# Attention's projections as float32 matmuls on two 64-row halves, from q and k also laid out transposed

## The chip, the cores and the metric

One core of a Trainium2 chip runs the whole kernel. The metric is device time in microseconds (us), the median of several runs. The core has a matrix engine (TensorE, PE in the rows; its weight loads are PEld), a vector engine (VectorE, DVE), a scalar engine (ScalarE, ACT), GpSimd (POOL) and SyncE (SP), whose queue issues most DMAs. Matmuls write to PSUM, eight banks of 128 x 512 float32; everything else lives in SBUF.

## The reference

Three stages, one after the other: attention with random features, a gated MLP over all tokens (MoE 1), and a top-1 mixture of eight experts (MoE 2).

```python
# attention: q, k, v [4, 8, 576, 64], omega [128, 64], float32
scale = 1 / sqrt(sqrt(64))
def phi(x):                                   # x = q * scale or k * scale
    h = einsum('bhsd,md->bhsm', x, omega) - sum(x * x, -1) / 2
    return exp(h - max(h, -1)) / sqrt(128)
kv = einsum('bhsm,bhsd->bhmd', k_p, v); z = sum(k_p, 2)
out = einsum('bhsm,bhmd->bhsd', q_p, kv) / (einsum('bhsm,bhm->bhs', q_p, z) + 1e-06)
# MoE 1: x [2304, 512]; w_a, w_b [512, 1536], w_out [1536, 512], given as float64
x = ((x @ w_a) * (x @ w_b)) @ w_out
# MoE 2: per token the expert with the largest cosine similarity,
#        out = gate * (relu(x @ w1[e]) @ w2[e]), w1 [8, 512, 1024], w2 [8, 1024, 512]
```

## The kernel before, in words

**Attention** is cut into 36 jobs, 18 of k and 18 of q. A job is 128 tokens x 8 (head, part) pairs, 1024 rows of 64 numbers; two neighbouring jobs share one load of 512 KB, and four jobs ("left") hold the last 64 tokens of two batch entries. `attention` runs over slots t; in slot t job t+2 is transposed and squared (`j_T`), job t+1 is projected and exponentiated (`j_proj`, `j_exp`), job t adds to the sums over keys (`j_kv`) or has its features transposed (`j_pT`), job t-1 is multiplied with these sums (`j_out`), and job t-2, where it ends a pair, is transposed for MoE 1 (`j_xT`). The loads of a job are called LEAD = 5 slots ahead.

In `j_T`, TensorE turns four blocks of 128 x 128 (L349), ScalarE copies them out scaled as float32r (L351), and VectorE makes the remainder (L352); GpSimd squares the tokens (L356) and folds the squares twice (L358). In `j_proj`, each of four blocks is multiplied with omega, two copies of it on a block diagonal of 128 x 256, as three float32r products (L595 to L597): both high parts, high with low, low with high. VectorE then takes the maximum of 512 columns (L377, two per job), adds the squares (L378) and forms the exponent's bias (L379), for each half of the job by itself; ScalarE makes eight exponentials (L390).

Beside attention, the float64 weights of MoE 1 are converted to float32 in 36 parts (L235, L236, L238, L240: ScalarE, VectorE, VectorE, GpSimd), 24 of them paced over the slots. **Early chunks:** ND = 5 of the 12 column chunks of MoE 1's first unit are multiplied inside attention, at slots TS = 28, 30, ..., 36 (step TD = 2), by `chunk_early` (splits of the weights, L574, L577) and `ab_mm` (24 matmuls; L609, L611).

**Order.** In attention a scheduler orders the instructions of each engine; each engine then runs its list strictly in that order, and SP too. From the first chunk after the early ones on, the order is as written. **Memory** in SBUF comes in slots of a few sizes: "ab" and "wo" (12 each: loads, converted weights), "c4" (4 of 4 KB: xT, xn, later split weights), "x6", "c2" and others. A new tile waits until the last reader of an older tile in its buffer is done.

The functions that the change touches, with the line numbers that the profile shows:

Of the kernel before, what the change touches and what calls it, by code (L numbers as in the profile page):

```python
# [20 lines left out]
VW = 66  # L21
# [18 lines left out]
ND = 5  # L40
TS = 28
TD = 2
# [38 lines left out]

class Later:
    """the engines, their instructions put in a queue for Kern.pump"""
# [17 lines left out]
class Kern:  # L101
    def __init__(s, tc, ctx, q, k, v, omega, w_a, w_b, w_out, emb, tau, w1, w2, cst, ids, ident, tri, out):
        s.tc, s.nc, s.out = tc, tc.nc, out
        s.q, s.k, s.v, s.omega = q, k, v, omega
# [22 lines left out]
    def pump(s, n):  # L127
        """the next n instructions of the queue, up to a barrier; a stage puts its own in its place"""
# [14 lines left out]
    # on-chip memory: slots of few sizes, shared by the phases  # L143
# [81 lines left out]
    def conv_ops(s):  # L225
        """float32 nearest to each float64 (in float32's range), a third of a chunk at a time"""
# [56 lines left out]
    def p0_consts(s):  # L283
        """omega^T twice on the diagonal, in two parts"""
        nc = s.nc
        bd = s.c2([128, 2, 128], F32, "bd")
        nc.vector.memset(bd, 0.0)
        pt = s.psum("O", "omT")
        nc.tensor.transpose(pt[:, :128], s.om2.rearrange("p a d -> p (a d)"), s.ident)
        for i in range(2):  # L290
            nc.vector.tensor_copy(out=bd[64 * i:64 * i + 64, i], in_=pt[64 * i:64 * i + 64, :128])
        s.omh = s.one([128, 256], F32R, "omh")
        s.oml = s.one([128, 256], F32R, "oml")
        s.split(s.omh, s.oml, bd.rearrange("p a m -> p (a m)"))
# [193 lines left out]
    def attention(s):  # L488
# [18 lines left out]
        for t in range(-2, J + 3):  # L507
# [15 lines left out]
            if c:  # L523
                s.hi_()
# [874 lines left out]
```

## Time and profile before

| | us |
|---|---|
| median of three runs | 920.87 (916.97 to 922.1) |
| profiled execution, span | 917.3 |
| TensorE busy in it | 847.3 (92%) |
| VectorE | 599.2 (65%) |
| ScalarE | 452.0 (49%) |
| GpSimd | 349.9 (38%) |
| TensorE's mean granted clock | 0.979 of 2.4 GHz |

The page gives no other time of the profiled execution than its span, which lies 3.6 us under the median and inside the spread of the runs. Busy shares over the whole span mix attention (some 200 us) with the two MoE stages, whose limits differ; the page's 40 slices show VectorE at 8 and 9 tenths in the first eight slices and at 3 to 8 after, TensorE at 9 nearly everywhere after them. A record of TensorE lasts longer than the distance to the next one, since matmuls overlap: the distance between two starts is what a matmul costs in a stream.

### The profile page before, as it was taken

The page shows a single profiled execution, that of the slowest core. Times are in us where ns is not written, and L with a number is a line of the kernel's source. Part 1 is how long each engine was busy: PE and PEld are TensorE (multiplying, and loading weights), DVE is VectorE, ACT ScalarE, POOL GpSimd, SP SyncE. Part 2 cuts the span into 40 slices and gives each one's busy share as a digit, 9 for nine tenths or more (in the row PEclk, how much of TensorE's full clock was granted, in tenths as well). Part 3 has the DMA queues.
Part 4 walks back from the last instruction along what each step waited for, and adds up shares of the span by engine and source line. Part 5 has one row for each costly group of instructions (what it writes and reads, how often), then busy time and mean ns, then how long its engine had stood idle before and what let it go on. Part 6 is the DMA issues. An engine that isn't in the chain of part 4 may idle for free. (4 is left out here: it accounts for less than half of the span.)

```text
span 917.3 us, 15916 instructions
## 1 busy us (share of the span) xinstructions
PE 847.3 (92%) x5784; PEld 763.8 (83%) x5784; DVE 599.2 (65%) x1295; ACT 452.0 (49%) x1039; POOL 349.9 (38%) x332
## 2 busy tenths in 40 slices
PE   7889897999899999999999999999899799998991
PEld 6778786898798899899889989989688698887880
DVE  6899999858956866874885687588547432225310
ACT  4789887665445546555555545655431321114210
POOL 6676877304315125222512421341404433333330
PEclk9999999999999999999999999999899899999996
DMA  9674853203200000000000004300214732122110
GB/s 235 183 199 123 240 152 121 74 8 118 114 1 0 36 1 1 1 36 1 1 36 1 1 0 103 117 1 37 60 55 142 262 98 64 50 62 63 61 48 24
DMA packets 68359, 67.20 MB, mean 73 GB/s; under 512 B 27552, under 2 KB 56608, under 8 KB 68096
## 3 DMA queue, kind: packets, MB, share of 16 engines
q1 hardware_dynamic: 62784, 52.90, 19.2%
q0 software_dynamic: 5440, 12.68, 4.6%
q8 instruction: 63, 1.03, 0.5%
q14 instruction: 72, 0.59, 0.2%
HBM read 55.88 MB, written 9.68 MB: 71 GB/s over the span
## 5 line engine op out<-in xcount | busy, mean ns | idle before, releaser
L660 POOL TENSOR_TENSOR trp<-y,en 128x512 f32<-128x512 f32 x60 | 89.2, 1508 | 138.2 <-ACT y L635 91.1
L1034 PE MATMUL p_h<-xth,w1t 128*128 128x256 f32 (+1 forms) x512 | 101.6, 294 | 8.4 <-DVE w2t L563 4.9
L562 ACT CAST hh<-h 128x384 fp32r<-128x384 f32 x72 | 36.9, 513 | 141.7 <-DVE h L611 141.7
L563 DVE TENSOR_TENSOR abl<-ab,abh 128x1024 fp32r<-128x1024 f32 x67 | 84.7, 1264 | 20.9 <-ACT abh L562 20.8
L597 PE MATMUL pB<-xuh,abl 128*128 128x384 f32 x288 | 96.9, 336 | 0.0
L390 ACT ACTIVATE p<-pj,nb 128x128 f32<-128x128 f32 x288 | 80.0, 397 | 26.0 <-DVE nb L379 14.8
L1034 PEld LDWEIGHTS p_h<-xth,w1t 128*128 128x128 f32 x512 | 83.4, 194 | 9.4 <-issue 9.2
L595 PE MATMUL pA<-xuh,abh 128*128 128x384 f32 x268 | 90.2, 336 | 0.0
L597 PE MATMUL pA<-xuh,abl 128*128 128x384 f32 x268 | 89.9, 335 | 0.3 <-DVE abl L563 0.3
L596 PE MATMUL pA<-xul,abh 128*128 128x384 f32 x268 | 90.0, 336 | 0.0
L595 PE MATMUL pB<-xuh,abh 128*128 128x384 f32 x268 | 89.5, 334 | 0.0
L596 PE MATMUL pB<-xul,abh 128*128 128x384 f32 x268 | 89.5, 334 | 0.0
L611 DVE TENSOR_TENSOR h<-pB,a 128x384 f32<-128x384 f32 x72 | 39.7, 551 | 69.5 <-PE pB L597 44.9
L1034 PE MATMUL p_h<-xtl,w1t 128*128 128x256 f32 (+1 forms) x256 | 75.0, 293 | 0.0
L653 DVE CUSTOM_DVE_ANT_0 trv<-y,en 128x512 bf16<-128x512 f32 x60 | 72.2, 1203 | 1.0
L627 PE MATMUL pO<-woh,hh 128*128 128x512 f32 x216 | 65.0, 409 | 7.7 <-ACT woh L562 7.7
L1014 ACT ACTIVATE hT<-p_h 128x512 fp32r<-128x512 f32 (+1 forms) x42 | 22.5, 537 | 98.2 <-PE p_h L1034 86.7
L562 ACT CAST abh<-ab 128x1024 fp32r<-128x1024 f32 x67 | 70.2, 1048 | 0.6 <-PE pB L596 0.6
L1019 DVE SCALAR_TENSOR_TENSOR hT<-p_h,hT 128x256 fp32r<-128x256 f32 (+2 forms) x52 | 25.2, 504 | 68.2 <-ACT hT L1014 47.4
L627 PE MATMUL pO<-woh,hl 128*128 128x512 f32 x216 | 63.8, 404 | 2.8 <-DVE hl L563 2.8
L563 DVE TENSOR_TENSOR hl<-h,hh 128x384 fp32r<-128x384 f32 x72 | 40.4, 561 | 34.8 <-ACT hh L562 34.8
L627 PE MATMUL pO<-wol,hh 128*128 128x512 f32 x216 | 62.7, 399 | 0.0
(233 smaller groups left out, 2142.4 us busy)
## 6 DMA issues: line engine op xcount, KB each, us to landing
stg<-in_moe_w_a_dram SPq DMA_DIRECT2D x12, 512.0 KB, 4.3
stg<-in_moe_w_b_dram SPq DMA_DIRECT2D x12, 512.0 KB, 3.4
stg<-in_moe_w_out_dram SPq DMA_DIRECT2D x12, 512.0 KB, 3.6
st<-in_moe_w_dram SPq DMA_DIRECT2D x12, 512.0 KB, 8.2
st<-in_moe_w_dram SPq DMA_DIRECT2D x24, 256.0 KB, 4.4
yd<-y SPq DMA_DIRECT2D x6, 792.0 KB, 3.7
v<-in_v_dram SPq DMA_DIRECT2D x16, 256.0 KB, 6.1
q<-in_q_dram SPq DMA_DIRECT2D x8, 512.0 KB, 5.1
```

The lines of the kernel that those rows point to most:

```text
L390: s.nc.scalar.activation(out=s.p_[j][:, 4 * half + n], in_=pj[:, n * M:n * M + M], func=ACTF.Exp, bias=nb[:, n:n + 1])
L562: s.nc.scalar.copy(out=hi, in_=src)
L563: s.nc.vector.tensor_tensor(out=lo, in0=src, in1=hi.bitcast(F32), op=ALU.subtract)
L595: mm(out=out, lhsT=ah, rhs=wh, start=st, stop=False)
L596: mm(out=out, lhsT=ah, rhs=wl, start=False, stop=False)
L597: mm(out=out, lhsT=al, rhs=wh, start=False, stop=sp)
L611: nc.vector.tensor_tensor(out=h, in0=pp[1][:, :N], in1=a, op=ALU.mult)
L627: s.nc.tensor.matmul(out=s.po[j], lhsT=a[:, j * 128:j * 128 + 128], rhs=b, start=st, stop=sp)
L653: nc.vector.tensor_tensor_reduce(out=tr, in0=y[:, j, :DM], in1=s.en[:, e], scale=1.0, scalar=0.0, op0=ALU.mult, op1=ALU.add, accum_out=dt[ ...
L660: nc.gpsimd.tensor_tensor(out=tr, in0=y[:, j, :DM], in1=s.en[:, e], op=ALU.mult)
L1019: nc.vector.scalar_tensor_tensor(out=v, in0=pv[:, a - k0:b - k0], scalar=0.0, in1=h, op0=ALU.max, op1=ALU.subtract)
L1034: return lambda: nc.tensor.matmul(out=out, lhsT=a, rhs=b, start=st, stop=sp, skip_group_check=True)
```

## The change

The host now hands over more: `laid` gives q and k as before by token (contiguous per partition), and also transposed (`qta`, `kta`, `qtb`, `ktb`): on partitions 0 to 63 the 64 numbers of each head's even tokens, on 64 to 127 those of the odd ones (for the left tokens: of even and odd heads), tokens along the row. v comes with its columns of ones, omega transposed, twice one below the other.

On the core the transposes, the float32r copies and their remainders, and omega's splits are gone. `j_proj` multiplies, for each of four blocks and each half r of the rows, `kt[64r:64r+64]` (64 x 128, stationary) with `omr[64r:64r+64]` (64 x 128, moving) as one native float32 matmul, the two halves into two PSUM banks. The bias is formed once for all eight rows of a job, after both maxima. The token tiles of q and k, needed for the squares only, now take c4 buffers. ND, TS and TD go from 5, 28, 2 to 6, 18, 3: early chunks at slots 18, 21, ..., 33. `ab_mm` writes its product over its input, and the last preparation of the expert embeddings comes after the conversion in a step, not before.

```diff
-ND = 5
-TS = 28
-TD = 2
+ND = 6
+TS = 18
+TD = 3
...
+def laid(q, k, v, omega):
...
+    def tr(x):
+
+        a = x[:, :, :512].reshape(B, H, 2, 128, 2, D).transpose(0, 2, 4, 5, 1, 3)
+        c = x[:, :, 512:].reshape(2, 2, 4, 2, 64, D).transpose(0, 3, 5, 2, 1, 4)
+        return np.ascontiguousarray(a.reshape(8, 128, H * 128)), np.ascontiguousarray(c.reshape(2, 128, 512))
...
+        s.omr = s.one([128, M], F32, "omr")
+        s.first = s.ab([128, H * 128], name="kt")
+        n = H * 64
+        nc.sync.dma_start(out=s.omr, in_=s.om)
+        nc.sync.dma_start(out=s.first[:, :n], in_=s.x_in["kt"][0][0, :, :n])
+        nc.sync.dma_start(out=s.first[:, n:], in_=s.x_in["kt"][0][0, :, n:])
         nc.sync.dma_start(out=s.ident, in_=ident)
...
+        s.nc.vector.tensor_scalar(out=s.omr, in0=s.omr, scalar1=SCALE, scalar2=None, op0=ALU.mult)
+
+    def load_part(s, what, where, i):
+        left = where == "left"
+        if (what, where, i) == ("kt", 0, 0):
             return s.first
...
+        src = s.x_in[what][1][i] if left else s.x_in[what][0][2 * where + i]
+        if what in "qk":
+            t = s.c4([128, src.shape[-1]], F32, what)
         else:
+            t = (s.wo if left else s.ab)([128, src.shape[-1]], name=what)
+        s.nc.sync.dma_start(out=t, in_=src)
         return t
...
-        for what in ("kv" if kind == "K" else "q"):
+        for what in (("kt", "k", "v") if kind == "K" else ("qt", "q")):
...
-        pt = s.psum("O", "pT")
-        for n in range(4):
-            nc.tensor.transpose(pt[:, n * 128:n * 128 + 128], x[:, n], s.ident)
-        t = s.c4([128, 2, 512], F32R, "xT")
-        s.hi_ = lambda: nc.scalar.activation(out=t[:, 0], in_=pt, func=ACTF.Copy, scale=SCALE)
-        s.lo_ = lambda: nc.vector.scalar_tensor_tensor(
-            out=t[:, 1], in0=pt, scalar=SCALE, in1=t[:, 0].bitcast(F32), op0=ALU.mult, op1=ALU.subtract)
...
+        pj = [s.psum("A", "pj") for _ in range(2)]
+        for n in range(4):
+            c = slice(n * 128, n * 128 + 128)
+            for r in range(2):
+                g = slice(64 * r, 64 * r + 64)
+                nc.tensor.matmul(out=pj[r][:, c], lhsT=t[g, c], rhs=s.omr[g], start=True, stop=True, skip_group_check=True)
+        return pj
...
+    def j_bias(s, j):
+
+        stt = s.nc.vector.scalar_tensor_tensor
+        mx = s.mx_.pop(j)
+        ss = s.sq_[j].rearrange("p (n r) -> p r n", r=2)
+        nb = s.t("nb", 4, [128, 2, 4], F32, "nb")
+        stt(out=mx, in0=ss, scalar=-SCALE * SCALE / 2, in1=mx, op0=ALU.mult, op1=ALU.add)
+        stt(out=nb, in0=ss, scalar=-SCALE * SCALE / 2, in1=mx, op0=ALU.mult, op1=ALU.subtract)
+        return nb
...
+            if b:
+                s.j_max(b, 0, pj)
                 fill()
+                s.j_ssq(b)
+                s.j_max(b, 1, pj)
+                nb = s.j_bias(b)
+                fill()
+                for half in range(2):
+                    s.j_exp(b, half, pj, nb)
...
-        h = s.c15([128, N], F32, "h")
-        nc.vector.tensor_tensor(out=h, in0=pp[1][:, :N], in1=a, op=ALU.mult)
-        return h
+        nc.vector.tensor_tensor(out=a, in0=pp[1][:, :N], in1=a, op=ALU.mult)
+        return a
```

How the order of instructions moves, at three places. First TensorE's list over a q job and a k job in the middle of attention, before (pT: transposes of k or q; pj: projections; ppT: transposes of the features; ou: products with the sums; kv: sums over keys):

```order
L597 MATMUL pj<-omh,xT 128x256 x2
L595 MATMUL pj<-omh,xT 128x256
L596 MATMUL pj<-oml,xT 128x256
L597 MATMUL pj<-omh,xT 128x256
L450 MATMUL ou<-kvs,pT 64x65 x8
L420 MATMUL kv<-v,p 64x65 x12
L450 MATMUL ou<-kvs,pT 64x65 x8
L420 MATMUL kv<-v,p 64x65 x12
L349 MATMUL pT<-ident_t,q 128x128 x4
L595 MATMUL pj<-omh,xT 128x256
L596 MATMUL pj<-oml,xT 128x256
L597 MATMUL pj<-omh,xT 128x256
```

Now, at a like place (pxT: transposes for MoE 1):

```order
L368 MATMUL pj<-omr,kt 128x128 x8
L438 MATMUL ppT<-ident_t,p 128x128 x8
L486 MATMUL pxT<-ident_t,xn 128x128 x8
L368 MATMUL pj<-omr,qt 128x128 x8
L455 MATMUL ou<-kvs,pT 64x65 x8
L425 MATMUL kv<-v,p 64x65 x8
L455 MATMUL ou<-kvs,pT 64x65 x8
L425 MATMUL kv<-v,p 64x65 x8
L368 MATMUL pj<-omr,kt 128x128 x8
```

The four transposes and twelve projections of a job have become eight projections on half the rows, which stand between full transposes and products on half the columns. The count at a row's end is that of the program; a float32 product is two rows in the trace.

Second, VectorE's list over a little more than one job in the middle, before (cv: conversion of weights; rr, xn: division of the result):

```order
L377 TENSOR_REDUCE mxh<-pj 128x4 x2
L378 SCALAR_TENSOR_TENSOR mxh<-ssq,mxh 128x4
L352 SCALAR_TENSOR_TENSOR xT<-pT,xT 128x512
L379 SCALAR_TENSOR_TENSOR nb<-ssq,mxh 128x4
L378 SCALAR_TENSOR_TENSOR mxh<-ssq,mxh 128x4
L238 SCALAR_TENSOR_TENSOR cv<-stg,cv 128x512
L379 SCALAR_TENSOR_TENSOR nb<-ssq,mxh 128x4
L236 TENSOR_SCALAR cv<-stg 128x512
L384 TENSOR_REDUCE ssq<-sq 128x8
```

Now:

```order
L374 TENSOR_REDUCE mxh<-pj 128x4 x2
L263 TENSOR_SCALAR cv<-stg 128x512
L382 SCALAR_TENSOR_TENSOR mxh<-ssq,mxh 128x8
L469 TENSOR_SCALAR rr<-ou 128x4
L383 SCALAR_TENSOR_TENSOR nb<-ssq,mxh 128x8
L265 SCALAR_TENSOR_TENSOR cv<-stg,cv 128x512
L470 RECIPROCAL rr<-rr 128x4
L469 TENSOR_SCALAR rr<-ou 128x4
L471 TENSOR_TENSOR xn<-ou,rr 128x2x128
```

The remainder (L352) is gone, and of four small operations with the squares two are left, each on eight columns; other work stands between them.

Third, SP's queue, near the last load of k. Before, with what each waits for (stg: float64 weights; DMAHW: an older DMA's queue entry):

```order
L220 DMA stg<-in_moe_w_b_dram 128x4x256 [waits DMAHW0_49,DVE_49,Activation_49]
L223 DMA stg<-in_moe_w_out_dram 128x1024 [waits DMAHW1_49,DVE_49,Activation_49]
L309 DMA q<-in_q_dram 128x8x128 [waits DMAHW2_49,PE_49]
L309 DMA k<-in_k_dram 128x8x128 [waits DMAHW3_49,PE_49,Pool_49]
L307 DMA v<-in_v_dram 128x8x64 [waits DMAHW4_49,PE_49,Pool_49]
L307 DMA v<-in_v_dram 128x8x64 [waits DMAHW5_49]
L220 DMA stg<-in_moe_w_a_dram 128x4x256 [waits DMAHW6_49,DVE_49,Activation_49]
```

Now:

```order
L323 DMA kt<-in_kta_dram 128x1024 [waits DMAHW6_49,PE_49]
L323 DMA v<-in_va_dram 128x1056 [waits DMAHW7_49,PE_49]
L247 DMA stg<-in_moe_w_a_dram 128x4x256 [waits DMAHW0_49,DVE_49]
L217 DMA cst_t<-in_cst_dram 128x161 [waits DMAHW1_49]
L247 DMA stg<-in_moe_w_b_dram 128x4x256 [waits DMAHW2_49,DVE_49,Activation_49]
L250 DMA stg<-in_moe_w_out_dram 128x1024 [waits DMAHW3_49,DVE_49,Activation_49]
L218 DMA ids_t<-in_ids_dram 128x36 [waits DMAHW4_49]
L247 DMA stg<-in_moe_w_a_dram 128x4x256 [waits DMAHW5_49,DVE_49,Activation_49]
L323 DMA k<-in_ka_dram 128x1024 [waits DMAHW6_49,Pool_49]
```

The token tile k, which used to be the matmul's operand and to be issued right behind q, now waits for GpSimd alone and stands behind four loads of weights; kt and v go ahead of them.

## Rows read from the trace of the kernel before

**Rows 1.** Windows: length, busy us PE PEld DVE ACT POOL, clock, DMA share, GB/s.

```profile
0.00:13.50 13.50, 8.51 (x37) 7.25 (x37) 7.21 (x18) 2.99 (x5) 6.75 (x13) 1.00 0.95 198
13.50:32.80 19.30, 17.50 (x231) 14.81 (x232) 14.60 (x44) 13.80 (x48) 13.82 (x20) 1.00 1.02 279
32.80:139.60 106.80, 95.40 (x1276) 85.92 (x1274) 105.37 (x293) 92.06 (x268) 79.69 (x85) 0.98 0.60 171
139.60:187.50 47.90, 41.84 (x447) 38.38 (x446) 43.68 (x107) 33.58 (x91) 22.67 (x22) 0.96 0.28 86
...
262.00:900.00 638.00, 612.76 (x3379) 553.38 (x3377) 373.89 (x749) 269.61 (x558) 206.60 (x174) 0.99 0.15 49
```

**Rows 2.** Timeline of ScalarE, jobs 5 and 28: start, us, instruction, idle before.

```profile
32.76 2.19 ACT L390 ACTIVATE p<-pj,nb 128x128 f32<-128x128 f32 x8
...
139.58 1.14 ACT L390 ACTIVATE p<-pj,nb 128x128 f32<-128x128 f32 x4 [0.56 <-DVE nb L379]
```

**Rows 3.** Groups by line, VectorE, 0 to 202.4: busy us, mean ns | idle before.

```profile
L352 DVE SCALAR_TENSOR_TENSOR xT<-pT,xT 128x512 fp32r<-128x512 f32 x36 | 24.4, 679 | 1.5 <-ACT xT L351 1.4
L379 DVE SCALAR_TENSOR_TENSOR nb<-ssq,mxh 128x4 f32<-128x4 f32 x72 | 24.1, 338 | 0.1
...
L378 DVE SCALAR_TENSOR_TENSOR mxh<-ssq,mxh 128x4 f32<-128x4 f32 x72 | 21.4, 300 | 0.0
...
L577 DVE TENSOR_TENSOR abl<-ab,aby 128x512 fp32r<-128x512 f32 x5 | 4.4, 888 | 0.0
L577 DVE TENSOR_TENSOR aby<-ab,aby 128x512 fp32r<-128x512 f32 x5 | 3.9, 774 | 0.3 <-ACT aby L574 0.3
L611 DVE TENSOR_TENSOR h<-pB,a 128x384 f32<-128x384 f32 x5 | 2.8, 552 | 11.0 <-PE pB L597 11.0
```

**Rows 4.** Line L379: ns least/median/most, first and last start, shape.

```profile
L379 DVE SCALAR_TENSOR_TENSOR nb<-ssq,mxh x72: 119/161/1241, 12.5 to 187.6; 128x4 f32<-128x4 f32 x72
```

**Rows 5.** Timeline of VectorE: the remainder and its successor.

```profile
182.87 0.68 DVE L352 SCALAR_TENSOR_TENSOR xT<-pT,xT 128x512 fp32r<-128x512 f32 x1
183.47 0.15 DVE L379 SCALAR_TENSOR_TENSOR nb<-ssq,mxh 128x4 f32<-128x4 f32 x1
```

**Rows 6.** Groups by line, ScalarE, 0 to 202.4: the copy of the transposes.

```profile
L351 ACT ACTIVATE xT<-pT 128x512 fp32r<-128x512 f32 x36 | 23.6, 656 | 3.9 <-PE pT L349 3.9
```

**Rows 7.** Timeline of TensorE: kv, an early chunk and a job, MoE 1's begin.

```profile
103.00 0.64 PE L420 MATMUL kv<-v,p 128*64 128x65 f32 x16
103.47 0.64 PE L450 MATMUL ou<-kvs,pT 128*64 128x65 f32 x16
...
175.51 0.42 PE L595 MATMUL pA<-xuh,aby 128*128 128x384 f32 x1
...
179.84 0.60 PE L349 MATMUL pT<-ident_t,q 128*128 128x128 f32 x4
180.19 0.37 PE L595 MATMUL pj<-omh,xT 128*128 128x256 f32 x1
...
181.58 0.28 PE L597 MATMUL pj<-omh,xT 128*128 128x256 f32 x1
181.79 0.69 PE L450 MATMUL ou<-kvs,pT 128*64 128x65 f32 x16
182.40 0.66 PE L433 MATMUL ppT<-ident_t,p 128*128 128x128 f32 x4
182.99 0.69 PE L450 MATMUL ou<-kvs,pT 128*64 128x65 f32 x16
...
202.48 0.42 PE L595 MATMUL pA<-xuh,abh 128*128 128x384 f32 x1
```

**Rows 8.** Waits of TensorE, 20 to 175 and after 200: us, times, longest.

```profile
PE pA L597 <- DVE aby L577: 3.3, 1, 3.3
...
PE pO L627 <- DVE hl L563: 2.8, 1, 2.8
```

**Rows 9.** DMA issues, 0 to 200: size, median us from issue to landing.

```profile
q<-in_q_dram SPq DMA_DIRECT2D x8, 512.0 KB, 5.1
```

More of the change, by code (lines that the diff above doesn't have):

```diff
@@ L354, in j_T @@
+        x = s.src[kind.lower(), where, i]
+        if where != "left":
+            x = x[:, 512 * (i % 2):512 * (i % 2) + 512]
         sq = s.t("trp", 2, [128, 8, D], F32, "sq")
-        sqb = sq.rearrange("p (n c) d -> p n (c d)", c=2)
-        nc.gpsimd.tensor_tensor(out=sqb, in0=x, in1=x, op=ALU.mult)
+        nc.gpsimd.tensor_tensor(out=sq.rearrange("p c d -> p (c d)"), in0=x, in1=x, op=ALU.mult)
         for w in (32, 16):
             nc.gpsimd.tensor_tensor(out=sq[:, :, :w], in0=sq[:, :, :w], in1=sq[:, :, w:2 * w], op=ALU.add)
-        s.xT_[j] = t
@@ new lines, in j_max @@
+    def j_max(s, j, r, pj):
+        if j not in s.mx_:
+            s.mx_[j] = s.t("mxh", 4, [128, 2, 4], F32, "mxh")
+        s.nc.vector.tensor_reduce(out=s.mx_[j][:, r], in_=pj[r].rearrange("p (h m) -> p h m", m=M), axis=AX.X, op=ALU.max)
+    def j_bias(s, j):
[6 more added lines that the diff above has]
+        return nb
@@ L385, in j_ssq, with j_exp @@
         s.sq_[j] = ss
-    def j_exp(s, j, half, pn):
-        pj, nb = pn[:2]
-        for n in range(4):
+    def j_exp(s, j, half, pj, nb):
+        for n in range(4 * half, 4 * half + 4):
+            m, r = divmod(n, 2)
             s.nc.scalar.activation(
-                out=s.p_[j][:, 4 * half + n], in_=pj[:, n * M:n * M + M], func=ACTF.Exp, bias=nb[:, n:n + 1])
+                out=s.p_[j][:, n], in_=pj[r][:, m * M:m * M + M], func=ACTF.Exp, bias=nb[:, r, m:m + 1])
     def j_kv(s, j, half):
@@ L399, in j_kv @@
             if where == "left":
+                v = v.rearrange("p (h d) -> p h d", d=VW) if n == 4 * half else v
                 s.kv_mm(2 * i, h, p[0:64, n], v[0:64, h])
@@ L488, in attention @@
     def attention(s):
-        for n in ("src", "xT_", "sq_", "p_", "later", "kvp", "kvn", "kvs", "pT_", "xn_"):
+        for n in ("src", "sq_", "p_", "mx_", "later", "kvp", "kvn", "kvs", "pT_", "xn_"):
             setattr(s, n, {})
@@ L518, in attention @@
                 s.j_T(c)
-            pj = [s.j_proj(b, half) for half in range(2)] if b else None
+            pj = s.j_proj(b) if b else None
             for f in s.xT_evac:
@@ L555, in attention @@
             if a:
-                for d in (s.xT_, s.sq_, s.p_):
+                for d in (s.sq_, s.p_):
                     d.pop(a)
@@ L1383 @@
     nc = bacc.Bacc("TRN2", target_bir_lowering=False, num_devices=1)
-    given = {}
+    given = laid(*(np.asarray(inputs[name]) for name in ("q", "k", "v", "omega")))
     for name in _INS:
```

108 lines of the change are left out of this document (28 added, 80 removed).

## The prediction

> **What bounds the kernel now.** I first cut the span into stretches with the table of windows [rows 1]. The cuts are where ScalarE begins the exponentials of attention's jobs 0, 5, 28 and 35 (the timeline shows the two in the middle, 23 jobs apart [rows 2]) and where the last attention matmul hands over to MoE 1, at 202.5 [rows 7]. From 262 on TensorE is busy 96% of the time, and little less between the two: a microsecond taken from its work, or from the time before 202.5, is a microsecond of the result. Before 202.5 it is not TensorE that sets the pace. From 32.8 to 139.6 VectorE is busy 105.4 of 106.8 us, TensorE 95.4, ScalarE 92.1, GpSimd 79.7. A job takes 106.8 / 23 = 4.64 us there, and VectorE's work is what fills it. From 139.6 to 187.5 VectorE is again the busiest (43.7 of 47.9), with TensorE close (41.8). In the last 15 us before 202.5 two early chunks of MoE 1 lie beside the end of attention.
>
> Next I read which VectorE work that is, from the groups by line [rows 3]. Of the instructions that a job needs, the change takes L352 (0.679 us) and half of L378 and L379 (0.300 and 0.338 each). The latter are 128x4 operations; L379 takes 0.161 in the median, but up to 1.24 [rows 4].
>
> **VectorE, removed.** Per job one L352 and two small ones go: 0.679 + 0.300 + 0.338 = 1.32 us. Records overlap their neighbours: L352 at 182.87 has its successor at 183.47, 0.60 us later for a record of 0.68 [rows 5]. So I take 0.07 off each: 1.1 us per job. The two that stay become 128x8; eight elements for four I cost at nothing, since the time of these is start-up and waiting, not elements. Were each longer by half of 0.161, it would be 0.16 us per job back. The memsets of v go too, and the preparation of omega at the start.
>
> **ScalarE, removed.** L351, 0.656 us per job [rows 6], about 0.6 net.
>
> **TensorE, removed and added.** In a run of TensorE's timeline [rows 7] the four transposes of a job take 180.19 - 179.84 = 0.35 us, and the twelve 128x256 projections 181.79 - 180.19 = 1.60: 1.95 per job go. The new ones are 8 native float32 matmuls of 64 x 128 stationary on 128 columns. The trace of before has no such shape. The nearest rows are the kv and ou products, float32 on 64-column halves: 8 of them in the program are 16 passes in the trace, so float32 takes two passes, and 16 passes go from 103.00 to 103.47, 0.029 us per pass of 65 columns. If row halves run side by side as these column halves do, 128 columns take 0.029 x 128 / 65 = 0.058, and 16 passes 0.92 us. If each waits for the other, the nearest row is a full-array float32 transpose of 128 columns, 4 in 182.99 - 182.40 = 0.59 with a change of shape in it, some 0.125 each: 16 make 2.0 us. I take 0.95, nearest to the products that are also two passes on half the array. Changes of shape: 181.58 to 181.79 is 0.21 where the eleven before it are 1.39 / 11 = 0.13 apart, so 0.08 each; now there are about five per pair of jobs where there were two or three, 0.1 us per job. Net TensorE per job: 1.95 - 0.95 - 0.1 = 0.9 less, or 0.15 more by the upper bound. The Trainium skill, TensorEngine Tiling (Array Packing), Key Properties, says that a change of tiling mode drains the engine, which speaks against rows mixed with columns like this; the trace agrees in kind, with 0.08 as its size, and a drain of a whole record (0.28) in each of five would make 0.5 us per job more.
>
> **GpSimd** keeps all its work (squares and their sums on it as before).
>
> **Moved: early chunks.** One costs TensorE 179.84 - 175.51 = 4.33 us; VectorE 0.888 + 0.774 + 0.552 = 2.2, some 2.0 net [rows 3, 7]; ScalarE two operations. Before, the five come at slots 28 to 36: three in 139.6 to 187.5, two after. Now six come at slots 18 to 33: three before job 28, three from there to job 35, none after.
>
> **Loads.** q and k come twice, 9.4 MB more, but the row pieces are 2 to 4 KB long. DMA is full only up to 32.8 us, at 198 and 279 GB/s [rows 1]. Up to job 5 the queue now has 5.0 MB ahead; at 279 GB/s 18 us, under the 25 that the work itself needs below. So I cost them at nothing there. Later the share was 0.60 and 0.28.
>
> **The sum, stretch by stretch, against the profiled 917.3 us.**
> - To 13.5: the two splits of omega and the transposes are gone; the chain is now k's landing, three operations of GpSimd, the bias. 10.5 us instead of 13.5: gain 3 (1 to 5).
> - Jobs 0 to 4, 19.3 us: TensorE 17.5 - 5 x 0.9 = 13, GpSimd 13.8, ScalarE 13.8 - 3 = 10.8, VectorE 14.6 - 5.5 = 9.1. I take 14.5: gain 4.8 (2 to 6).
> - Jobs 5 to 27, 106.8 us: VectorE 105.4 - 23 x 1.1 + 3 x 2.0 = 86; TensorE 95.4 - 23 x 0.9 + 3 x 4.33 = 88; ScalarE 92.1 - 23 x 0.6 = 78 and six operations more; GpSimd 79.7. Four engines are within 10% of each other, so none will be busy 99% as VectorE was. With TensorE 93% busy, 95 us: gain 12 (6 to 18).
> - Jobs 28 to 34, 47.9 us: TensorE 41.8 - 7 x 0.9 = 35.5, VectorE 43.7 - 7.7 = 36, the same three chunks. The old wait of 3.3 us for a chunk's split [rows 8] can come again, and on SP the load of k for job 28 now stands behind weight loads that wait for the conversion. I take 43: gain 5 (1 to 10).
> - From job 35: two chunks (8.7 us) leave 6.3; what stays is a chain (transposes, copy, product, reciprocal, transposes) that nothing covers any more. I take 9: gain 6.
> - After: one chunk fewer, 4.3 less, but its cover goes. 12 conversions now fall on four steps, not five, and VectorE is the later one there already (TensorE waits 2.8 us for hl [rows 8]). I take 3 us back: gain 1.3.
>
> Together 32 us: 917.3 - 32 = 885.3. The median of the runs, 920.87, is 3.6 above the span; so 889.
>
> **The rivals.**
> *The row halves do not run side by side.* For it: no row here shows two row halves at once. Against: column halves do run so [rows 7]. At 2.0 us per job TensorE has 0.15 more work per job than before; jobs 5 to 27 then have 95.4 + 3 + 13 = 112 us of TensorE records, and gain nothing; the jobs before and after keep about 3 + 1 + 1, the end 5, the rest 1: 10 us, 911. The Trainium skill, TensorE: Matmul & The Clock Gate, section LDWEIGHTS (loading the stationary operand), says that a load of weights takes as long as its columns, whatever the rows; an estimate by its figure, 128 / 1.2 = 107 ns, makes 16 loads one after the other 1.7 us, near this rival; no row here shows loads of this shape.
>
> *GpSimd's collisions eat the gain.* For it: L379 runs from 0.119 to 1.24 us [rows 4], so VectorE's small operations wait for something; GpSimd's work stays, in less time, at 80 of 95 us in the middle. If that middle takes 101 and each later stretch 2 more: 32 - 6 - 6 = 20 gained, 901.
>
> *The four engines overlap better.* TensorE and VectorE then set 89, 38 and 7 in the three last stretches of attention: 6 + 5 + 2 more, 45 gained, 876.
>
> *Slower: the four c4 buffers.* The token tiles of q and k now share these with xn; 16 loads wait on SP for GpSimd's squares of an older tile, and kt, v and the weights queue behind them. If a load is issued too late for its job, a landing of 5.1 us [rows 9] stands open. Seven of them cancel the gain; ten give 51 - 32 = 19 us more, 940. Against: each load is called five jobs ahead, some 20 us, and a buffer comes round after 5.3 slots.
>
> **How the numbers follow.** The forecast, 889, has 0.50 (by itself 878 to 900); better overlap, 876, 0.19; the halves in turn, 911, 0.12; collisions, 901, 0.13; late loads, 940, 0.06. The range, 868 to 912, leaves out the last and the far ends of the others. 0.5%, 4.6 us, is about what a measurement can tell (the three runs spread 5.1 us). Faster by more: all of the first, second and fourth, most of the third: 0.90. Same 0.04, slower 0.06.
>
> **What would show it.** The new projections: 16 passes in about 1 us, pairs starting together (right), or 2 us (the first rival). VectorE in the middle stretch below 95% busy and a job under 4.2 us. No L351 and L352. The exponentials of job 35 near 163 us and MoE 1 at about 172 instead of 202.5. TensorE waiting for kt or qt from DMA, or GpSimd for k or q, by more than 10 us in total, would be the last rival. The forecast is wrong if MoE 1 begins later than 185 or if the time after it grows by more than 6 us.

## The result and the profile after

The changed kernel takes 932.16 us (median of 4 runs, 929.89 to 932.53), the kernel before 919.77 in runs on the same chip: a ratio of 1.012, with a 95% interval of 1.0091 to 1.015. It is slower, and the forecast was 889. Of all runs one, of lean_chunks, counts as slow (1.7% above the fastest of its kernel), and it is left out below. The profiled execution has a span of 930.3 us, 13.0 more than before's 917.3, and a mean clock of 0.954 (0.979 before).

The table of windows of the changed kernel (columns as in [rows 1]), cut where ScalarE begins jobs 0, 5, 28 and 35; the last line is the middle of MoE 1 and 2:

```profile
0.00:14.10 14.10, 3.79 (x32) 3.52 (x32) 5.35 (x12) 1.49 (x3) 6.57 (x13) 1.00 0.84 305
14.10:32.90 18.80, 17.94 (x234) 14.70 (x236) 9.23 (x22) 11.39 (x42) 11.72 (x17) 1.00 1.03 406
32.90:159.80 126.90, 104.62 (x1346) 90.98 (x1345) 103.91 (x243) 85.78 (x251) 88.65 (x95) 0.85 0.56 196
159.80:203.10 43.30, 38.65 (x450) 33.67 (x448) 26.16 (x73) 28.86 (x82) 11.91 (x12) 0.92 0.15 50
...
275.00:914.00 639.00, 614.81 (x3385) 555.40 (x3383) 374.22 (x750) 269.12 (x558) 205.67 (x173) 0.99 0.16 49
```

VectorE's bias, which answers to [rows 3]: the two operations of 128x8, of which there are half as many as of 128x4 before, and the sum of squares, in the groups by line before 210 us (busy us, mean ns | idle before):

```profile
L383 DVE SCALAR_TENSOR_TENSOR nb<-ssq,mxh 128x8 f32<-128x8 f32 x36 | 15.9, 444 | 0.6
...
L382 DVE SCALAR_TENSOR_TENSOR mxh<-ssq,mxh 128x8 f32<-128x8 f32 x36 | 12.1, 337 | 0.2
L388 DVE TENSOR_REDUCE ssq<-sq 128x8 f32<-128x128 f32 x36 | 10.1, 279 | 15.7 <-POOL sq L352 14.9
```

They are 0.44 and 0.34 us, 0.14 us more together than the two of before that the forecast took for them; that the third operation waits for GpSimd (14.9 us) was not in it at all. The cuts are these rows of ScalarE's timeline, which answer to [rows 2] (start, us, instruction, idle before):

```profile
14.10 4.24 ACT L394 ACTIVATE p<-pj,nb 128x128 f32<-128x128 f32 x16 [11.87 <-DVE nb L383]
32.94 2.17 ACT L394 ACTIVATE p<-pj,nb 128x128 f32<-128x128 f32 x8 [0.17 <-DVE nb L383]
...
159.84 2.18 ACT L394 ACTIVATE p<-pj,nb 128x128 f32<-128x128 f32 x8 [0.69 <-DVE nb L383]
...
203.18 2.17 ACT L394 ACTIVATE p<-pj,nb 128x128 f32<-128x128 f32 x8
```

Jobs 5 to 27 hold the loss: 126.9 us for 106.8, although VectorE and TensorE are busy only 82% there (104 and 105 of 127) and the others less; TensorE's 105 hold passes at half clock (the mean clock is 0.85 there). No engine is the bound any more; they wait for each other. Against before, stage by stage: to job 0 +0.6 us, jobs 0 to 4 -0.5, jobs 5 to 27 +20.1, jobs 28 to 34 -4.6, from job 35 to the last transposes of attention (15.2 us before, 7.0 now) -8.2, from there to MoE 1's second unit of 384 tokens (58.1 before, 64.6 now) +6.5, the rest -0.9. Together 13.0.

Who waits for whom, from the waits of the changed kernel before 210 us (engine, line, released by: total, times, longest):

```profile
ACT p L394 <- DVE nb L383: 45.3, 18, 11.9
...
PE kv L425 <- ACT p L394: 28.8, 9, 6.6
POOL ab L267 <- ACT ab L262: 15.3, 6, 4.8
...
DVE ssq L388 <- POOL sq L352: 14.9, 8, 5.0
POOL sq L350 <- DMA k<-in_ka_dram: 11.4, 2, 7.2
...
POOL sq L350 <- DVE ssq L388: 8.0, 6, 2.5
```

The same view of the kernel before, to 202.5 us:

```profile
ACT p L390 <- DVE nb L379: 14.8, 15, 5.8
POOL sq L356 <- DVE ssq L384: 13.6, 9, 2.4
...
PE kv L420 <- ACT p L390: 1.9, 2, 1.2
```

Before, GpSimd waits for VectorE. Now VectorE waits for GpSimd as well, ScalarE for VectorE, and TensorE for ScalarE. The timeline of all engines at one such place of the changed kernel shows such waits behind each other, in what is called the ring below:

```profile
78.79 0.64 PE L425 MATMUL kv<-v,p 128*64 128x65 f32 x16
...
80.37 1.30 ACT L262 ACTIVATE ab<-stg 128x512 int32<-128x512 uint32 x2
...
81.19 1.27 POOL L267 TENSOR_TENSOR ab<-cv,ab 128x512 int32<-128x512 int32 x1 [4.75 <-ACT ab L262]
...
82.41 1.05 POOL L350 TENSOR_TENSOR sq<-k 128x512 f32<-128x512 f32 x1
...
84.05 1.16 PE L368 MATMUL pj<-omr,qt 64*128 64x128 f32 x16
...
85.14 0.69 PE L455 MATMUL ou<-kvs,pT 128*64 128x65 f32 x16
...
86.31 1.67 POOL L352 TENSOR_TENSOR sq<-sq 128x128 f32<-128x128 f32 x3
...
86.82 0.29 DVE L388 TENSOR_REDUCE ssq<-sq 128x8 f32<-128x128 f32 x1 [5.03 <-POOL sq L352]
...
87.02 1.28 DVE L374 TENSOR_REDUCE mxh<-pj 128x4 f32<-128x512 f32 x2
...
90.39 0.41 DVE L383 SCALAR_TENSOR_TENSOR nb<-ssq,mxh 128x8 f32<-128x8 f32 x1
...
90.84 2.17 ACT L394 ACTIVATE p<-pj,nb 128x128 f32<-128x128 f32 x8 [4.94 <-DVE nb L383]
...
91.26 1.26 PE L425 MATMUL kv<-v,p 128*64 128x65 f32 x16 [5.43 <-ACT p L394]
```

ScalarE's part of a weight conversion (L262) comes late; GpSimd stands 4.75 us at its own part (L267), with squares queued behind it. VectorE stands 5.03 us at a sum of squares (L388), with two maxima queued behind it whose projections were done by 81.5. The bias, the exponentials and TensorE's products follow. TensorE's 16 passes of kv took 0.64 us at 78.79; the 16 at 91.26, after 5.43 us of idling, take 1.26, and the granted clock's record is 0.5 from 87.8 to 94.7. Such pieces at half clock sum to 44 us between 20 us and attention's end (6.8 before).

### The profile page after: what moved, and what is told of

It reads as the page before. It is cut to its first block, busy times and chain, and to the rows that moved or that the text cites. A ratio compares the mean times of both kernels' runs of the same rounds, so it can differ in the third digit from the quotient of the medians.

```text
span 930.3 us, 15725 instructions
## 1 busy us (share of the span) xinstructions
PE 840.9 (90%) x5783; PEld 751.6 (81%) x5783; DVE 571.2 (61%) x1175; ACT 432.6 (46%) x1002; POOL 348.1 (37%) x332
## 5 line engine op out<-in xcount | busy, mean ns | idle before, releaser
L560 ACT CAST hh<-a 128x384 fp32r<-128x384 f32 x72 | 36.9, 513 | 144.6 <-DVE a L608 138.4
L608 DVE TENSOR_TENSOR a<-pB,a 128x384 f32<-128x384 f32 x72 | 39.7, 552 | 80.4 <-PE pB L595 55.3
L594 PE MATMUL pB<-xul,abh 128*128 128x384 f32 x264 | 88.3, 334 | 0.0
L1011 ACT ACTIVATE hT<-p_h 128x512 fp32r<-128x512 f32 (+1 forms) x42 | 22.2, 536 | 104.6 <-PE p_h L1031 68.2
L425 PE MATMUL kv<-v,p 128*64 128x65 f32 (+1 forms) x640 | 40.1, 266 | 28.8 <-ACT p L394 28.8
```

The costliest lines, as they stand in the source:

```text
L425: nc.tensor.matmul(out=out[m, c:c + D + 1], lhsT=p[:, m], rhs=v[:, :D + 1], start=(n == 0), stop=(n == 19), skip_group_check=True)
L560: s.nc.scalar.copy(out=hi, in_=src)
L594: mm(out=out, lhsT=ah, rhs=wl, start=False, stop=False)
L608: nc.vector.tensor_tensor(out=a, in0=pp[1][:, :N], in1=a, op=ALU.mult)
```

## The experiments

All times are medians; ratios are to the kernel before on the same chip. "Half clock" is the sum of the pieces with a granted clock of 0.5 from 20 us to attention's end, "attention's end" that of its last transposes, "second unit" where MoE 1 begins it; these, and the stages, are from the timelines and clock records of the profiled executions. The runs were made on several chips, where the kernel before takes 917.6 to 920.8 us, so a difference of a few us between two kernels is read from their ratios.

| kernel | us | ratio (95%) | jobs 5-27 | attention's end | second unit | half clock |
|---|---|---|---|---|---|---|
| before | 919.8 | 1 | 106.8 | 202.7 | 260.8 | 6.8 |
| changed | 932.2 | 1.0091-1.0150 | 126.9 | 210.2 | 274.9 | 44.4 |
| proj_alone | 923.9 | 1.0034-1.0081 | 118.7 | 208.5 | 266.2 | 45.4 |
| sched_alone | 933.8 | 1.0138-1.0191 | 131.6 | 214.7 | 277.4 | 17.1 |
| bias_bank | 927.0 | 1.0066-1.0128 | 127.3 | 207.0 | 271.8 | 41.6 |
| sq_early | 932.0 | 1.0096-1.0166 | 129.3 | 210.6 | 275.3 | 44.8 |
| kv_late | 917.7 | 0.9964-1.0010 | 115.2 | 200.4 | 258.0 | 44.4 |
| no_sq | 899.5 | 0.9762-0.9840 | 99.8 | 183.4 | 241.3 | 20.5 |
| conv_late | 920.3 | 0.9994-1.0042 | 113.3 | 205.2 | 262.7 | 32.9 |
| sq_t | 914.0 | 0.9944-0.9978 | 110.9 | 198.7 | 256.5 | 34.1 |
| sq_mm | 932.1 | 1.0117-1.0181 | 135.0 | 230.1 | 287.1 | 71.7 |
| sq_mm_kv | 910.6 | 0.9896-0.9950 | 109.5 | 201.2 | 258.7 | 27.3 |
| pace | 926.0 | 1.0059-1.0121 | 123.9 | 206.3 | 266.0 | 27.3 |
| before_no_sq | 907.0 | 0.9827-0.9911 | 99.6 | 187.6 | 245.8 | 3.4 |
| no_sq_kv | 889.2 | 0.9627-0.9702 | 94.6 | 173.9 | 233.7 | 20.5 |
| lean | 884.9 | 0.9586-0.9696 | 88.3 | 166.1 | 223.8 | 3.4 |
| lean_chunks | 886.6 | 0.9561-0.9671 | 103.5 | 172.3 | 232.4 | 6.8 |
| lean_loads | 879.4 | 0.9513-0.9621 | 86.5 | 165.3 | 223.1 | 13.7 |
| lean_kv | 885.8 | 0.9550-0.9651 | 88.7 | 167.6 | 225.8 | 10.2 |

**The two halves of the change.** proj_alone:

```diff
-ND = 6; TS = 18; TD = 3      # and next(en) behind the conversions again
+ND = 5; TS = 28; TD = 2
```

> The new projections with the early chunks of before (five, from slot 28, one in two slots) and before's order after attention. Theory A (the chain of one job: projections, both maxima, bias, exponentials is too long and the engines wait for each other): jobs 5 to 27 still take well over 100 us although no chunk lies in them, the waits of ScalarE for the bias stay at 30 us or more, and the time is 915 to 930 us. Rival B (the earlier chunks and the work that they leave behind cost the time): jobs 5 to 27 take 95 us or less, and the time is 895 to 910 us. Rival C (GpSimd's squares come late): as A, with VectorE's wait for the squares at 10 us or more.

sched_alone is the kernel before with the opposite edit.

> The old projections with the early chunks of the change (six, from slot 18, one in three slots) and its order after attention. Theory A: the schedule by itself is worth little, 915 to 925 us. Rival B: the schedule by itself costs what the whole change costs, 928 to 938 us, with the part after attention no shorter than before's although it has a chunk fewer. Rival C: as A.

The projections alone cost 4 us, the schedule alone 14. Both theories had a part: without one chunk in them, jobs 5 to 27 still take 118.7 us with the new projections (A), and in the old kernel, whose VectorE had nothing to spare, three chunks make the stretch 24.8 us longer (B), where the forecast charged 4.33 us of TensorE each. Rival B's second sign came too: behind attention sched_alone takes 62.7 us to the second unit, with a chunk fewer than before's 58.1. The two losses don't add: on the new schedule the new projections cost nothing (932.2 against 933.8). The waits of proj_alone to 203 us are those of the changed kernel, without its chunks:

```profile
ACT p L394 <- DVE nb L383: 52.4, 19, 10.3
PE kv L425 <- ACT p L394: 30.8, 11, 5.4
...
DVE ssq L388 <- POOL sq L352: 19.2, 10, 5.0
```

**The chain of one job.** bias_bank, on the changed kernel, forms the bias of a bank behind its own maximum:

```diff
-    max(0); ssq; max(1); nb = bias(both); exps of all eight
+    ssq; for r in range(2): max(r); nb = bias(r); exps of bank r
```

> The changed kernel with the bias formed for one bank of four head blocks as soon as its maximum is there, and that bank's four exponentials behind it (two more VectorE instructions of about 0.2 us per job); the exponentials and the products of a half follow the banks. Theory A: the exponentials of a job start about 1 us earlier, ScalarE's wait for the bias falls from 45 us to 25 or less, and the time falls by 8 to 25 us, to 907 to 924. Rivals B and C: 928 to 936 us, since the chunks and the squares stand where they stood.

The expectation failed. By the medians it gave 5 us, by the ratios 2, with intervals that overlap; ScalarE's wait for the bias stayed at 45.7 us (to 203 us), and jobs 5 to 27 at 127.3. kv_late, on proj_alone:

```diff
-c, b, a, p, p2 = (get(t + n) for n in (2, 1, 0, -1, -2))
+c, b, a, p, p2 = (get(t + n) for n in (2, 1, -1, -2, -3))
```

> proj_alone (new projections, early chunks as before the change; 923.9 us) with the products of keys and values, the transposes of the features and all that follows them one slot later, so that TensorE never asks for exponentials that were begun in the slot before. Theory A (the chain of one job is longer than the slots leave it, and TensorE stands at the head of its queue for exponentials): TensorE's wait for exponentials falls from 25.1 us between 33 and 190 us to under 8, its clock stays up, and the time falls to 900 to 914 us. Rival C (GpSimd's squares set the pitch): the wait moves to TensorE's projections or to VectorE, 920 to 926 us. Rival D (the lower clock sets the pitch by itself): 918 to 925 us.

TensorE's wait for exponentials before kv goes as expected (25.1 to 1.3 us between 33 and 190), the gain is 6 us: less than theory A's. The clock did not stay up (0.86 in the mean there), and TensorE is busy only 123.1 of these 157 us: it now waits for other work of VectorE, as rival C has it. From the waits of kv_late, 33 to 190 us:

```profile
DVE ssq L388 <- POOL sq L352: 13.3, 8, 3.4
...
PE ou L455 <- DVE mxh L374: 6.1, 1, 6.1
PE ppT L438 <- DVE xn L471: 5.6, 4, 2.3
...
PE kv L425 <- ACT p L394: 1.3, 1, 1.3
```

So something else holds the pitch too.

**The squares.** sq_early, on the changed kernel, moves both the squares and their sum a slot ahead:

```diff
+if c3: s.j_T(c3)          # job t + 3, was t + 2
+if c: s.j_ssq(c)          # job t + 2, was t + 1
```

> The changed kernel with each job's squares formed on GpSimd one slot earlier and summed on VectorE one slot earlier. Rival C: VectorE's wait for the squares (14.9 us before job 35) falls below 4 us and the time falls by 8 to 15 us, to 917 to 924. Theory A: the wait goes, but the chain of the job stays, 925 to 932 us. Rival B: 930 to 934 us.

No gain; VectorE still waits 10.0 us for squares between 33 and 190. The sum moved with the squares, so its distance behind them stayed: the run doesn't tell. (The squares have two buffers in all runs; a third was not tried.) no_sq, on proj_alone:

```diff
-for what in (("kt", "k", "v") if kind == "K" else ("qt", "q")):
+for what in (("kt", "v") if kind == "K" else ("qt",)):
-    squares on GpSimd; ssq = their sum
+    ssq = a tile of zeros
```

> proj_alone without the squares: their token loads, GpSimd's work and VectorE's sum are left out, the bias is formed from a zero in their place, so the features are scaled otherwise. Rival C: jobs 5 to 27 fall from 108 us to under 95 and the time to 900 to 912 us. Theory A: 6 to 10 us of the waits go with VectorE's wait for the squares (13.6 us), 914 to 920 us. Rival D: 920 to 925 us.

24 us, half a us better than rival C's range; jobs 5 to 27 fall from 118.7 (not 108, as the expectation has it) to 99.8, not under 95. (The square is subtracted from the projections and from their maximum, so it cancels but for rounding; the expectation's word on scaling was wrong.) More than late squares went with this edit. In no_sq the two operations of the bias (to 185 us; its lines differ) are shorter than the 0.337 and 0.444 us of the changed kernel:

```profile
L378 DVE SCALAR_TENSOR_TENSOR mxh<-ssq,mxh 128x8 f32<-128x8 f32 x36 | 10.2, 283 | 0.3
...
L379 DVE SCALAR_TENSOR_TENSOR nb<-ssq,mxh 128x8 f32<-128x8 f32 x36 | 6.9, 191 | 0.6
```

That is 0.31 us per job in the middle of the chain, some 11 us over 36 jobs: beside GpSimd's instructions they stand still (last section). VectorE's sum, 0.28 us per job, is gone too. How the 24 us divide between these and squares that come late, no run separates. sq_t keeps the work and drops the loads:

```diff
-x = s.src[kind.lower(), where, i]
+x = s.src[kind.lower() + "t", where, i]
```

> proj_alone with the squares formed from the transposed tile that is there anyway, so that the second load of q and k (by tokens) goes and GpSimd's and VectorE's work on squares stays as it was. It folds over tokens in place of features, so the features are scaled otherwise. Theory C1 (GpSimd's work on squares, between its conversions, sets the pitch; without squares and their loads the kernel took 899.5 us): most of the 24 us stays lost, 915 to 922 us. Theory C2 (the second load of q and k, some 9 MB in the first 120 us, sets it): 898 to 908 us.

10 us of the 24 (9 by the ratios), a little under C1's range and far from C2's, so the work on the squares has the larger part and the loads have one. conv_late, on proj_alone, gives GpSimd's step of a conversion out one conversion later:

```diff
-nc.gpsimd.tensor_tensor(out=c, in0=t, in1=c, op=ALU.add)
+if i: add()               # that of conversion i - 1
+add = lambda t=t, c=c: nc.gpsimd.tensor_tensor(out=c, in0=t, in1=c, op=ALU.add)
```

> proj_alone with GpSimd's last step of each weight conversion given out one conversion later, so that the squares behind it on GpSimd's queue need not wait for ScalarE's part. Rival C (a ring of queues: ScalarE's conversion step behind the exponentials, GpSimd's step behind that, the squares behind it, the bias behind those): GpSimd's wait for ScalarE (11.1 us) and VectorE's for the squares (13.6 us) fall by more than half and the time falls by 5 to 12 us, to 912 to 919 us. Theory A: 921 to 925 us, since the exponentials then wait for something else.

4 us, a little under the range: VectorE's wait for squares falls only from 13.6 to 8.5, and GpSimd's wait for ScalarE (33 to 190 us) rises from 11.1 to 14.7. So the link of the ring that goes through the conversions is seen in the timeline above, but is not shown to set the pitch. sq_mm sums the squares on TensorE:

```diff
-two folds on GpSimd, tensor_reduce on VectorE
+for n in range(4): matmul(out=pq[:, 2*n:2*n+2], lhsT=sq[:, 128*n:128*n+128], rhs=bd2)
+vector.tensor_copy(out=ss, in_=pq[:, :8])
```

> proj_alone with the squares taken from the transposed tile (no second load of q and k), one GpSimd instruction of about 1.05 us per job in place of three of 2.7 us, and their sums over features on TensorE: four products per job with a two-column constant, 0.4 to 1 us; VectorE copies eight numbers. It computes the same as the reference. C1: 898 to 908 us. C2: the same, and then sq_t is near it. If neither squares nor loads are the cause but the mere removal of work in no_sq: 912 to 922 us.

> sq_mm with the products of keys and values and the transposes of features one slot later, as in kv_late (which gave 6 us by itself). If GpSimd's lateness and the short chain of a job are two causes, the gains add: 4 to 6 us under sq_mm. If the short chain only mattered because the squares came late: within 2 us of sq_mm.

sq_mm is 8 us slower than proj_alone, which no expectation had, though GpSimd is busy 62.6 us in place of 99.8. From the windows 33 to 203 of proj_alone and of sq_mm (one line each; the clock is the number behind POOL's):

```profile
33.00:203.00 170.00, 139.36 (x1824) 119.90 (x1823) 128.93 (x321) 117.50 (x342) 99.84 (x115) 0.88 0.48 166
```

```profile
33.00:203.00 170.00, 155.72 (x1814) 141.11 (x1811) 113.39 (x280) 104.18 (x309) 62.62 (x53) 0.79 0.39 129
```

The sums stand on TensorE between the projections and the bias, 0.96 us per job at full clock, and lengthen the chain; with one more slot (sq_mm_kv) 21 us come back, far more than either expectation, and the kernel is faster than before (0.9896 to 0.9950) although it keeps the squares. Why TensorE's clock falls most here, with more to do, is not settled.

**The clock.** warm adds products that nobody reads:

```diff
+for _ in range(2): matmul(out=po[:, 384:512], lhsT=ident, rhs=ident, start=True)   # and into kv's bank
```

> proj_alone with four products per slot of a constant with itself into columns that nobody reads (some 1.1 us of TensorE per job at full clock, about what the removed transposes took), ahead of the products of keys and values and of the outputs. Rival D (TensorE has less to do, so its clock falls, and the lower clock takes back the gain): the granted clock between 33 and 190 us rises from 0.87 to 0.95 or more and the time falls by 4 us or more, to under 920 us. Theory A: the waits stay, TensorE has more to do, 922 to 935 us.

957.4 us (ratio 1.0384 to 1.0496). The added products also change the result, as far as can be told through the sums of keys and values that share their bank (last section), so only attention is compared: it ends at 224.5 us, 16 later than in proj_alone. The clock between 33 and 190 us rises only from 0.87 to 0.91, short of the 0.95 that the test needed, so warm does not decide on rival D. lean (below) does: 3.4 us at half clock, with less work for TensorE than before (busy 80.5 us in jobs 5 to 27, 95.4 before). Less work by itself does not lower the clock. The dips come where TensorE stands idle, whatever it waits for: kv_late, nearly without waits for exponentials but busy only 78% of 33 to 190 us, keeps its 44.4 us at half clock. What the half clock costs by itself, no run separates.

**Does the change pay without squares?** The kernel before without them:

```diff
-    squares on GpSimd; s.j_ssq(b)
+    s.sq_[j] = a tile of zeros
```

> The kernel before without the squares of q and k (they cancel in exact arithmetic: the maximum is taken after the square is subtracted): GpSimd's three instructions and VectorE's sum of each job go, the loads stay, since its transposes need them. Theory G (before, VectorE was the bound and GpSimd's squares were hidden; after the change they are not): only VectorE's 0.28 us per job comes back, 908 to 914 us, and no_sq (899.5 us) is faster by 9 to 15 us, which is what the new projections are worth by themselves. Rival H (the squares hold up both kernels alike): 893 to 900 us, and the new projections are worth nothing.

907.0 against 899.5, ratios of 0.9869 and 0.9801 whose intervals just overlap. Without squares the new projections pay 6 to 8 us, by the ratios and by the medians. Taking the squares out gives the kernel before 12 us, 1 us more than theory G's range, and the new projections twice that. In the kernel before the squares are not late, since VectorE idles 0.1 us ahead of its sum; their cost there is read as VectorE's own work, the sum and, again, the small operations. Rows of before, then of before_no_sq (to 185 us):

```profile
L384 DVE TENSOR_REDUCE ssq<-sq 128x8 f32<-128x128 f32 x36 | 9.6, 270 | 0.1
```

```profile
L377 DVE SCALAR_TENSOR_TENSOR nb<-ssq,mxh 128x4 f32<-128x4 f32 x72 | 18.9, 265 | 0.1
...
L376 DVE SCALAR_TENSOR_TENSOR mxh<-ssq,mxh 128x4 f32<-128x4 f32 x72 | 13.2, 185 | 0.0
```

The last two are 0.338 and 0.300 us in the kernel before [rows 3]. Next the chain, on no_sq:

> no_sq (899.5 us) with products of keys and values and transposes of the features one slot later, as in kv_late. If the short chain of a job is a cause of its own: TensorE's remaining wait for exponentials (13.7 us between 33 and 190 us) falls under 5 and the time to 888 to 895 us. If it was only a consequence of the late squares: 897 to 902 us.

And lean, with four VectorE instructions per job (two maxima, two for the bias) as no_sq has, but each bank's bias right behind its maximum:

```diff
-max(0); max(1); two scalar_tensor_tensor of 128x8; exps of all eight
+for r in range(2): max(r); nb = -max; exps of bank r        # no squares, no q and k by tokens
```

> proj_alone without squares and token loads, and the bias of each bank of four blocks is the negated maximum, formed by one VectorE instruction behind that bank's maximum, with the bank's four exponentials behind it; early chunks as before the change. If the chain of a job is a cause of its own: 887 to 895 us. If not: 895 to 899 us, for the removed VectorE work alone.

> lean with products of keys and values and transposes of the features one slot later. If bias by bank and one more slot cure the same wait: 882 to 888 us, since TensorE waits only 5.1 us for exponentials in lean. If they are two causes, as kv_late's 6 us and no_sq_kv's 10 us suggest: 873 to 880 us.

Each cure gives 10 to 15 us (no_sq_kv, lean), both together nothing more (lean_kv): one cause, the chain. lean is 2 us better than its range. In lean the table of windows and the waits of 33 to 165 us show what the forecast had expected, TensorE busy 91% and hardly waiting (the window runs 37 us past attention's end; in jobs 5 to 27 alone TensorE is busy 80.5 of 88.3 us):

```profile
33.00:203.00 170.00, 154.56 (x1879) 134.38 (x1880) 133.21 (x315) 130.15 (x354) 45.55 (x39) 0.98 0.42 141
```

```profile
ACT p L381 <- DVE nb L369: 8.4, 10, 3.8
...
PE kv L412 <- ACT p L381: 5.1, 2, 3.8
```

lean_loads is lean with no_sq's edit of the loads undone.

> lean (884.9 us) with the second loads of q and k put back, into the buffers that they have in the changed kernel, where nobody reads them. If the loads cost by themselves (they delay the loads that TensorE needs, above all at the start, where they stand between kt and the next tiles on SP's queue): 890 to 897 us. If they cost only through the squares that wait for them: 883 to 887 us.

879.4, under both ranges: the second loads cost nothing that can be measured when no square waits for them, although sq_t gained 10 us.

**After attention.** pace, on the changed kernel:

```diff
-next(en, None)            # ahead of the conversions; now behind them
-... NPRE + (3 * KF - NPRE) * (n + 1 - ND) // (KF - 2 - ND)
+... NPRE + (3 * KF - NPRE) * (n + 1 - ND) // 5
```

> The changed kernel (932.2 us) with the last 12 weight conversions after attention spread over five steps of MoE 1 in place of four, and the expert embeddings' step behind them as before the change. Theory E (conversions pressed into the first steps after attention keep VectorE from the splits that TensorE waits for): the stretch from attention's end to the second unit falls from 64.6 us to 58 to 61, the time to 925 to 929 us. Rival F (the early chunks leave fewer products to hide the same VectorE work, however it is spread): 64 us still, 930 to 934 us.

TensorE's waits behind attention in the changed kernel (203 to 275 us), which answer to [rows 8], and in pace (203 to 266):

```profile
PE pO L624 <- DVE hl L561: 7.2, 3, 4.3
...
PE pA L595 <- DVE abl L561: 3.5, 1, 3.5
```

```profile
PE pO L624 <- DVE hl L561: 4.7, 3, 2.1
...
PE pA L595 <- DVE abl L561: 0.4, 1, 0.4
```

Theory E holds for the stretch, which falls from 64.6 to 59.7 us. The time falls by 6 us by the medians and by 3 by the ratios, whose intervals overlap (attention ends 3.9 us earlier as well, which the edit was not meant for). Do the chunks pay without squares?

> lean with the change's six early chunks from slot 18 (one in three slots) and the conversions after attention over five steps as in pace. If the early chunks cost what they cost in the changed kernel whatever the projections do (pace against proj_alone: 2 us slower): 1 to 4 us over lean. If they only cost while the squares hold up the jobs: 2 to 5 us under lean, for the chunk that attention hides.

No difference from lean can be told: 886.6 against 884.9, ratios of 0.9616 and 0.9641, with intervals that overlap. In the profiled executions, attention ends 6.2 us later for one chunk more, and the stretch after it is 60.1 against 57.7 us although it has that chunk fewer. So no gain of the forecast's kind is seen, and the choice between the two expectations stays open.

lean and the others without squares are faster than the kernel before and the changed one; they leave out the squares, which cancel.

## Why the prediction was wrong

- *The new projections' own price was right.* Row halves run side by side: in the single records two passes start 0.007 us apart and the next two 0.11 later, and 16 passes go from 84.05 to 85.14, 1.09 us for the forecast's 0.95. The first rival (2 us) falls, and with it the estimate of 1.7 us from the Trainium skill, TensorE: Matmul & The Clock Gate, LDWEIGHTS (loading the stationary operand): loads and passes together took 1.09. The loads start in pairs too, one pair in 0.11 us. VectorE's and ScalarE's instructions are gone as counted.
- *Jobs 5 to 27, 95 us, is the step that failed:* "Four engines are within 10% of each other, so none will be busy 99% as VectorE was. With TensorE 93% busy, 95 us". It summed busy times and took for granted that queues keep TensorE supplied. It took 126.9, and the runs take this apart: 118.7 without the three chunks (proj_alone), 99.8 without squares as well (no_sq), 88.3 with the bias by bank besides (lean). With VectorE no longer the place where all work piles up, the wait from a job's projections over two maxima, one bias for both and eight exponentials to TensorE's products stood open, as kv_late, no_sq_kv and lean show (6, 10 and 15 us of the whole time). The busy times of the sum were off as well: VectorE 103.9 for 86, TensorE 104.6, partly at half clock, for 88. MoE 1 begins at 209.6, past the 185 that the prediction had set as its sign of being wrong.
- *GpSimd, which "keeps all its work" and entered the sum by its busy time alone, failed.* In the trace of before GpSimd waits for VectorE; the prediction did not ask what would wait for GpSimd once that was over. The squares and their loads cost 24 us in proj_alone; the squares cost 12 in the kernel before, there as work of VectorE. The rival on GpSimd had the engine, 12 us, and collisions of single instructions. The collisions are there (some 11 us in the chain, as no_sq shows); what it did not have are squares that come late (14.9 us of VectorE's waits).
- *To job 0, 10.5 us, failed* at 14.1: k's landing was in the chain, as written, but the load stood behind kt on SP's queue, and GpSimd's first square waits 7.2 us for it. In sq_t, where squares read kt, job 0 begins at 9.9. The sign set for the last rival (GpSimd waiting for k by over 10 us) came by the letter, 11.4 us, of which 7.2 are this start. Late loads by themselves are not the cause, since lean_loads pays nothing for them; through the squares that wait for them they have a part (sq_t).
- *Jobs 0 to 4, 14.5 us, failed* at 18.8: on TensorE's queue job 0's kv stands among job 2's projections, which are done at 21.3, and VectorE waits 4.9 us for them. In lean it is 13.8.
- *Early chunks in attention at 4.33 us of TensorE each.* In the changed kernel three of them make jobs 5 to 27 8.2 us longer than in proj_alone, less than the forecast's 13; in lean 15.2, in the old kernel 24.8. The sum had no term for the jobs that a chunk's splits delay on VectorE. That they cost less in the changed kernel because its engines stood idle anyway is argued, not shown.
- *Jobs 28 to 34, 43 us, and the end, 9 us, came out* at 43.3 and 7.0, the first in part by luck: VectorE is busy 26.2 us in it where the sum had 36, TensorE 38.7, at a clock of 0.92, where it had 35.5.
- *After attention, a gain of 1.3, failed:* 6.5 lost. The mechanism was named (12 conversions on four steps), the size was not: 3 us were charged, 10.8 came (6.5 and the 4.3 of a chunk fewer), 4.9 of which pace gives back. What keeps the rest is open.

That lean comes near the forecast's 889 (884.9) is chance in good part: it has no squares and no early chunk in jobs 5 to 27, which take 88.3 us; with three chunks there they take 103.5 (lean_chunks), where the sum had 95.

## What to carry to other kernels

A sum of busy times predicts an engine-bound stretch; once the full engine is relieved, follow one item of work through all queues and add up its latency, since that can set the pitch next. Slack of an engine that waits for the bound (GpSimd here) is not slack after the bound has gone: look what stands behind its waits in its own queue. And when two edits go in together, time each alone: here both lost against the kernel before.

## What the runs showed of the hardware

- Float32 products on row halves run side by side, at 1.09 us for 16 passes of 128 columns (0.068 each), and two passes start 0.007 us apart.
- A product with two columns costs nearly what one with 128 does: in sq_mm_kv 8 passes take 0.96 us (60.68 to 61.64), 8 passes of transposes of 128 columns 1.00 (65.07 to 66.07).
- TensorE's clock fell to half behind idle stretches of it, whatever it waited for: 44 us in the changed kernel, where it waits for exponentials, and 44 in kv_late, where it hardly does; 3.4 in lean, which gives it less work than before but keeps it busy 91% of 33 to 170 us. In sq_mm, with 71.7 us, this account is not enough.
- VectorE's small operations stand still beside GpSimd's instructions. L382 takes 0.168 us in the median and up to 1.146. Of the changed kernel's 72 operations of the bias (to 210 us) 26 take over 0.3 us; each of them begins while an instruction of GpSimd runs and ends 0.02 to 0.03 us after that one (a pair of rows stands below). Conversions do this as squares do: in no_sq, without squares, the longest is 1.241 us. The Trainium skill, SBUF — State Buffer, Who interferes with whom, says that the two engines hold a pair of ports one at a time for a whole instruction; the trace agrees.
- In warm the kernel's result changed although the added products wrote only columns that nobody reads, some of them in the bank in which the sums of kv run. The Trainium skill, PSUM — Partial Sum Buffer, The four PSUM rules, says that a starting product clears the marks of the whole bank, so that the next product overwrites in place of adding; the run agrees, but was not made to test it and does not show the sums themselves.

The pair, from the timeline of the changed kernel (a weight conversion of GpSimd, 92.23 to 93.50, and the bias, 92.56 to 93.53):

```profile
92.23 1.28 POOL L267 TENSOR_TENSOR wo<-cv,wo 128x512 int32<-128x512 int32 x1
...
92.56 0.97 DVE L382 SCALAR_TENSOR_TENSOR mxh<-ssq,mxh 128x8 f32<-128x8 f32 x1
```
